# A scan and two expert layers on one core: a tile table after 24 blocks, eight first tiles half by half, and weight conversions tied to results

## The chip, the cores and the metric

The kernel runs on one core of a Trainium2 chip. The metric is device time in microseconds (us), the median of several runs. The engines named below are TensorE (PE, with its weight loads PEld), VectorE (DVE), ScalarE (ACT), GpSimd (POOL) and SyncE (SP). Each works through its own queue in order, and "SPq" or "ACTq" marks a transfer that the engine issues.

## The reference

Three steps follow one another over 10112 tokens of 256 numbers (two sequences of 5056). The first is a gated scan along the tokens; the other two are layers of eight experts in which each token goes to one expert.

```
f = lower_bound + (1 - lower_bound) * sigmoid(f_logit)
h[t] = f[t] * h[t-1] + (1 - f[t]) * x[t]              # along 5056 tokens
# layer 1: the expert is argmax of cosine(x, expert_emb) / tau
# layer 2: the expert is argmax of x @ w_gate
out[rows of e] = gate * (relu(x[rows of e] @ w1[e]) @ w2[e])   # w1: 256x1024, w2: 1024x256
```

## The kernel before

**Blocks and chunks.** The tokens are 79 blocks of 128. A chunk is two blocks, and there are 40. For each chunk the kernel loads `xf` (512 KB), forms the gate on ACT (tanh, then a scale and a bias on ACT or POOL), runs the scan on DVE (`p_scan`: one pass over 128x512 and two scans over 128x256), turns the result round on PE into two PSUM tiles `yt` (`p_mm`) and writes rows in two half-precision parts (`p_hi` on ACT, `p_lo` on DVE). Two chunks make a group of four blocks, a quad. For a quad small instructions choose the expert of each row (`p_top`, `p_rank`, `p_slot`, `p_up`), and four indirect transfers of POOL scatter the rows to a table in DRAM, ordered by expert (`p_put`, `X<-row,sl`).

**Tiles and units.** A tile is 128 rows of one expert. A checkpoint after so many blocks computes on DVE which tiles are sure to be full by then, and writes the numbers into `tab`; `cps` lists the blocks after which this is done (16, 32, 48 and 64, and once more at the end). The number of tiles known after 16, 24 and 32 blocks is 9, 17 and 25. A tile is computed in two units, one for each half of the 1024 hidden columns. A unit is a first matmul `mm1` (24 matmuls into `hps`), its result taken out of PSUM by ACT and then by DVE (`evac`, tile `hT`, below simply the result of the unit), and a second matmul `mm2` (12 matmuls into `ops`), which stands three units later in the order (`lag`). Each unit of a tile that is computed half by half loads its own transposed rows `xT`, into one of four buffers.

**Halves and weights.** The first `g0` tiles run half by half: first their first halves, one after the other, then their second halves. ACT adds the partial sums aside (`acc`). So units 0 to g0-1 need only the first-half weights. Weights arrive as 512 KB pieces in single precision, one for each expert, half and matrix, and are split into two half-precision parts: `w_hi` on ACT, then `w_lo` on DVE (four of the first pieces by PE and ACT, `wd`). In the rows W_0_102 is the first half of the first weights, W_1_103 the second half of them, W_0_104 the first half of the second weights, W_1_105 the second half of those. Pieces wait for their conversion in parts of these arrays that aren't used yet, or in three buffers `ws`. `w1` says at which unit the conversion of the second halves begins.

**Order.** Every step of chunks, weights and tiles is put at a unit number (a slot, below zero ahead of unit 0) with a priority; SP's queue then keeps the order in which the steps were written, and a scheduler orders the other engines up to unit 17. `hold` and `rates` give the first slot of each chunk. PSUM holds six buffers that `yt`, `wd`, `hps` and `ops` use in turn.

Of the kernel before, what the change touches and what calls it, by code (L numbers as in the profile page):

```python
# [14 lines left out]
ALU = mybir.AluOpType  # L15
# [9 lines left out]

CFG = {'cps': (16, 32, 48, 64),
 'g0': 4,
 'swap': 21,
# [9 lines left out]
 'gdve': 0,  # L38
 'wpe': (4, 0),
 'yg': (0, 0),  # L40
 'man0': ('SP',),
# [3 lines left out]
 'hold': (8, -9),  # L45
 'rates': ((17, 2), (99, 4)),
 'alias': 8,
 'mans': 17,
# [15 lines left out]
 'sc': (0, 26),  # L64
 'w1': (-8, 0.8),
 'w1s': (20, 0.8),
# [58 lines left out]
def scan_moe_moe_kernel(ctx, tc, xf, emb, cst, tmp, w1a, w2a, w1b, w2b, out, seq, cfg=CFG):  # L125
# [59 lines left out]
    def stt(eng, out, in0, s, in1, op0, op1, **kw):  # L185
        assert eng is V
        return eng.scalar_tensor_tensor(out=out, in0=in0, scalar=s, in1=in1, op0=op0, op1=op1, **kw)  # L187
# [526 lines left out]

    ring = {}

    wreg = [T.alloc_register(f"wa{i}") for i in range(16)]
# [66 lines left out]
    def evac(t, h):  # L784
        hps = t.pop("hps")
        hT = hp.tile([P, 8, P], F16, name="hT", tag="hT", bufs=LAG + 2)
        hh = hT.rearrange("p (a c) q -> p a (c q)", a=2)
        A.activation(out=hh[:, 0], in_=hps, func=ACTF.Relu)  # L788
        stt(V, hh[:, 1], hps, 0.0, hh[:, 0], ALU.max, ALU.subtract)
        t["hT", h] = hT  # L790
# [254 lines left out]
    s0 = {}  # L1045
    s = cfg["start"]
    for c in range(NCH):
        if c == cfg["hold"][0]:
            s = cfg["hold"][1]
        s0[c] = int(s)  # L1050
        s += next(r for n, r in cfg["rates"] if c < n)
    first = min(s0.values())
    for c in range(NCH):
# [8 lines left out]
        if 2 <= c < cfg["alias"]:  # L1062
            at(first - 2 + (c - 2) // 2, 2, p_load, c)
        elif c >= 2:
            pa("load", p_load, c)
# [29 lines left out]
    wps = {}  # L1095

    def wstep(load, hi, lo, lo2):
        def w_done(item):
# [6 lines left out]
        if lo is not None:  # L1105
            t = wbuf.pop(lo)
            nlo[0] += 1
            i, k = nlo[0], (cfg["wpe"] + (0, 0))[(nlo[0] - 1) // 16]
            if (i * k) // 16 != ((i - 1) * k) // 16:
                wps[lo] = (w_sub(lo, t), t)  # L1110
            elif 16 < i <= 32 and tablast:
                with tc.issue_after(tablast[0]):
                    w_lo(lo, t)
                w_done(lo)
            else:
                w_lo(lo, t)
                w_done(lo)
        if hi is not None:
            w_hi(hi, wbuf[hi])
        if load is not None:  # L1120
# [272 lines left out]
```

## Time and profile before

| what | value |
|---|---|
| median of 3 runs | 1062.96 us (1060.74 to 1066.65) |
| time of the profiled execution | 1052.77 us |
| span from its first to its last instruction | 1050.9 us |
| PE busy | 996.1 us, 95% of the span |
| DVE, ACT, POOL busy | 602.3, 529.2, 407.8 us |

The span is 1.87 us shorter than the time of the same execution, and that execution was 10.19 us faster than the median of the runs. A row of a timeline gives the start, the busy time, the engine, the line and the operation with its output and inputs; in square brackets stands how long the engine was idle before it and what ended that. Busy times of neighbours overlap a little, so the distance from one start to the next is the better price of an instruction in a full queue. "Granted clock" (PEclk) is the share of TensorE's full clock, 1.00 for 2.4 GHz and 0.5 for 1.2 GHz.

### The profile page before, as it was taken

How to read it: one execution, taken by the hardware profiler on the slowest of the kernel's cores; microseconds unless marked ns; L12 is line 12 of the kernel's file. 1: busy time of each engine (PE TensorE's matmuls, PEld its weight loads, DVE VectorE, ACT ScalarE, POOL GpSimd, SP SyncE). 2: the span in 40 equal slices, each digit the busy share in tenths (PEclk: the TensorE clock that was granted, in tenths of full speed). 3: DMA queues.
4: the chain of work that ended last, by engine and by line, in shares of the span. 5: the costliest groups of instructions: out<-in, count | busy, mean ns of one | idle time of the engine just before them, and what ended most of it. 6: DMA issues, size and time to landing. Idle time of an engine off the chain costs nothing. (4 is left out here: it accounts for less than half of the span.)

```text
span 1050.9 us, 36737 instructions
## 1 busy us (share of the span) xinstructions
PE 996.1 (95%) x13267; PEld 932.6 (89%) x13267; DVE 602.3 (57%) x1927; ACT 529.2 (50%) x1301; POOL 407.8 (39%) x666
## 2 busy tenths in 40 slices
PE   5557999999999999999999999999999999999997
PEld 4436889999999999999998999999999999999997
DVE  7988877787778777665449778443222222222221
ACT  6978555665655565665346466443333333333332
POOL 5834645666666565332002550243222222222222
PEclk9967999999999999999999999999999999999999
DMA  9798436777677673875479699653322222222220
GB/s 352 244 342 209 132 59 120 144 136 130 124 127 127 152 125 94 195 196 149 62 170 205 123 197 267 117 103 72 52 52 53 52 53 48 45 50 44 47 51 31
DMA packets 195612, 132.69 MB, mean 126 GB/s; under 512 B 169601, under 2 KB 172558, under 8 KB 195440
## 3 DMA queue, kind: packets, MB, share of 16 engines
q1 hardware_dynamic: 172384, 60.18, 29.7%
q10 hardware_dynamic: 11200, 38.62, 14.7%
q0 software_dynamic: 11856, 31.51, 11.7%
q8 instruction: 118, 1.93, 0.8%
q14 instruction: 54, 0.44, 0.2%
HBM read 58.89 MB, written 38.85 MB: 93 GB/s over the span
## 5 line engine op out<-in xcount | busy, mean ns | idle before, releaser
L780 PE MATMUL hps<-xT,W 128*128 128x128 f16 x7968 | 504.9, 220 | 6.9 <-DVE hT L187 3.1
L802 PE MATMUL ops<-W,hT 128*128 x3984 | 489.3, 272 | 1.6 <-ACT acc L806 0.9
L780 PEld LDWEIGHTS <-W 128*128 x7968 | 475.6, 98 | 16.0 <-issue 6.3
L187 DVE SCALAR_TENSOR_TENSOR hT<-hps,hT 128x512 f16<-128x512 f32 x332 | 228.6, 688 | 318.4 <-ACT hT L788 315.7
L802 PEld LDWEIGHTS <-hT 128*128 128x128 f16 x3984 | 374.3, 98 | 41.4 <-issue 2.0
L788 ACT ACTIVATE hT<-hps 128x512 f16<-128x512 f32 x332 | 198.0, 596 | 303.2 <-PE hps L780 284.0
L970 POOL DMA_INDIRECT out<-osum,ti x83 | 81.1, 977 | 291.4 <-ACT osum L966 189.5
L948 POOL DMA_INDIRECT X<-trow,tsl x83 | 97.1, 1170 | 53.2 <-DVE tsl L187 18.0
L638 POOL DMA_INDIRECT X<-row,sl x79 | 92.8, 1174 | 55.1 <-issue 37.7
L966 ACT ACTIVATE osum<-ops,exr 128x256 f32<-128x256 f32 x62 | 29.3, 473 | 47.0 <-PE ops L802 44.8
L195 POOL TENSOR_TENSOR lf<-exr,us 128x2 f32<-128x2 f32 (+1 forms) x42 | 9.7, 231 | 102.6 <-DMA W<-WD 44.0
L187 DVE SCALAR_TENSOR_TENSOR W<-ws,W 128x1024 f16<-128x1024 f32 x34 | 41.5, 1220 | 8.7 <-ACT W L373 8.7
L373 ACT ACTIVATE W<-ws 128x1024 f16<-128x1024 f32 x35 | 37.1, 1060 | 12.5 <-DMA ws<-w2b 8.6
L825 ACT ACTIVATE trow<-osum 128x256 f16<-128x256 f32 x83 | 34.9, 420 | 16.0 <-DMA X<-trow,tsl 7.6
L492 DVE TENSOR_TENSOR_SCAN xf<-xf 128x256 f32<-128x256 f32 (+3 forms) x64 | 42.8, 710 | 0.1
L507 PE MATMUL yt<-cs,xf 128*128 128x128 f32 x126 | 28.3, 303 | 15.2 <-DVE xf L492 10.2
L814 ACT ACTIVATE osum<-ops 128x256 f32<-128x256 f32 x58 | 22.2, 382 | 38.3 <-PE ops L802 38.3
L187 DVE SCALAR_TENSOR_TENSOR trow<-osum,tsc,trow 128x256 f16<-128x256 f32 x83 | 36.7, 481 | 4.1 <-ACT trow L840 3.2
L187 DVE SCALAR_TENSOR_TENSOR xf<-xf 128x512 f32<-128x512 f32 (+1 forms) x32 | 21.8, 681 | 26.7 <-POOL xf L192 19.9
L547 ACT ACTIVATE row<-yt,sc 128x256 f16<-128x256 f32 x79 | 33.5, 481 | 6.5 <-DVE sc L192 6.5
L840 ACT ACTIVATE trow<-osum,tsc 128x256 f16<-128x256 f32 x62 | 28.1, 500 | 16.5 <-DVE tsc L192 14.9
L187 DVE SCALAR_TENSOR_TENSOR row<-yt,sc,row 128x256 f16<-128x256 f32 x79 | 36.0, 472 | 0.2 <-ACT row L547 0.2
(149 smaller groups left out, 929.2 us busy)
## 6 DMA issues: line engine op xcount, KB each, us to landing
xf<-xf ACTq DMA_DIRECT2D x28, 512.0 KB
ws<-w1b ACTq DMA_DIRECT2D x16, 512.0 KB
ws<-w2b ACTq DMA_DIRECT2D x16, 512.0 KB
W<-w1a SPq DMA_DIRECT2D x11, 512.0 KB
W<-xf SPq DMA_DIRECT2D x8, 512.0 KB
ws<-w2a ACTq DMA_DIRECT2D x8, 512.0 KB
WD<-wq SPq DMA_DIRECT2D x8, 512.0 KB
W<-WD SPq DMA_DIRECT2D x8, 512.0 KB
```

The costliest lines, as they stand in the source:

```text
L187: return eng.scalar_tensor_tensor(out=out, in0=in0, scalar=s, in1=in1, op0=op0, op1=op1, **kw)
L373: A.activation(out=hi, in_=src, func=ACTF.Copy, scale=64.0)
L492: V.tensor_tensor_scan(out=t[:, k, lo:hi], data0=t[:, 2 + k, lo:hi], data1=t[:, k, lo:hi], initial=init, op0=ALU.mult, op1=ALU.subtract)
L547: A.activation(out=p["row"][:, o + i, 0:D], in_=yv(d["yt"][i]), func=ACTF.Copy, scale=p["sc"][:, o + i:o + i + 1])
L638: x_write(0, G.indirect_dma_start(out=X[0], out_offset=IndirectOffsetOnAxis(ap=p["sl"][:, i, 0:1], axis=0), in_=p["row"][:, i, :].bitcast( ...
L780: T.matmul(out=hps[:, c, :], lhsT=w, rhs=xt[:, a, :], start=(n == 0), stop=(n == 5))
L788: A.activation(out=hh[:, 0], in_=hps, func=ACTF.Relu)
L802: T.matmul(out=o, lhsT=hT[:, a + k, :], rhs=w[:, b * D:(b + 1) * D], start=(first and k == 0 and n == 0), stop=(last and k == 3 and n == 2))
L825: A.activation(out=d["row"][:, i, D:2 * D], in_=t["O"], func=ACTF.Square, scale=0.25, accum_out=d["ss"][:, i:i + 1])
L948: x_write(1, G.indirect_dma_start(out=X[1], out_offset=IndirectOffsetOnAxis(ap=sl[:, i, 0:1], axis=0), in_=d["row"][:, i].bitcast(I32), in ...
L966: A.activation(out=r, in_=o, func=ACTF.Copy, scale=ex0[:, 0:1])
L970: i = ins_of(G.indirect_dma_start(out=out, out_offset=IndirectOffsetOnAxis(ap=ti, axis=0), in_=r, in_offset=None, bounds_check=N - 1, oob_ ...
```

## The change

Five things are edited. (1) A checkpoint after 24 blocks is added, so that the table comes in steps of 9, 8 and 8 tiles where it came in steps of 9 and 16. (2) Eight tiles instead of four run half by half, so units 0 to 7 use the first-half weights and units 8 to 15 the second-half ones. (3) The conversion of the second halves begins four slots later, and the pieces of W_1_105 but the first are put behind results: the piece of expert e not ahead of the result of unit e - 2, or of unit 0. (4) Chunks 8 to 11 are loaded at slots -18, -17, -12 and -10; before, the slots were -11, -9, -7 and -5. (5) Chunks 12 to 20 begin at slots 0, 2, 5, 8, 11, 14, 17, 19 and 22; before, at -1, 1, 3, 5, 7, 9, 13, 17 and 21.

```diff
-CFG = {'cps': (16, 32, 48, 64),
- 'g0': 4,
+CFG = {'cps': (16, 24, 32, 48, 64),
+ 'g0': 8,
+ 'wbe': 2,
+ 'first': {12: 0, 13: 2, 14: 5, 15: 8, 16: 11, 17: 14, 18: 17, 19: 19, 20: 22, 21: 25},
+ 'loads': {8: -18, 9: -17, 10: -12, 11: -10},
- 'w1': (-8, 0.8),
+ 'w1': (-4, 0.8),
+    evs = []
-        A.activation(out=hh[:, 0], in_=hps, func=ACTF.Relu)
-        stt(V, hh[:, 1], hps, 0.0, hh[:, 0], ALU.max, ALU.subtract)
+        i = A.activation(out=hh[:, 0], in_=hps, func=ACTF.Relu)
+        evs.append((ins_of(i), ins_of(stt(V, hh[:, 1], hps, 0.0, hh[:, 0], ALU.max, ALU.subtract))))
-        s0[c] = int(s)
+        s0[c] = cfg["first"].get(c, int(s))
+        elif c in cfg["loads"]:
+            at(cfg["loads"][c], 2, p_load, c)
+    def behind(item, eng, other=None):
+        m, which, h, e = item
+        if (m, which, h) == (0, 1, 1) and e:
+            other = evs[max(0, e - cfg["wbe"])][eng is V]
+        return tc.issue_after(other) if other is not None else ExitStack()
-                with tc.issue_after(tablast[0]):
+                with behind(lo, V, tablast[0]):
-            w_hi(hi, wbuf[hi])
+            with behind(hi, A):
+                w_hi(hi, wbuf[hi])
```

On SP's queue, at the start of the program, the loads stood thus before (`xf` is a chunk, `w1a` and `w2a` are weight pieces):

```order
L360 DMA W_1_103<-w1a 128x1024 x8
L360 DMA W_1_103<-w2a 128x1024 x4
L451 DMA xf<-xf 128x1024
L360 DMA W_1_103<-w2a 128x1024
L360 DMA ws<-w2a 128x1024
L451 DMA xf<-xf 128x1024
L360 DMA ws<-w2a 128x1024
L360 DMA W_1_105<-w1a 128x1024
L360 DMA ws<-w2a 128x1024
```

Now the same place of SP's queue reads:

```order
L363 DMA W_1_103<-w1a 128x1024 x4
L454 DMA xf<-xf 128x1024
L363 DMA W_1_103<-w1a 128x1024
L454 DMA xf<-xf 128x1024
L363 DMA W_1_103<-w1a 128x1024 x3
L363 DMA W_1_103<-w2a 128x1024 x3
L454 DMA xf<-xf 128x1024
L363 DMA W_1_103<-w2a 128x1024 x2
L454 DMA xf<-xf 128x1024
L363 DMA ws<-w2a 128x1024 x2
```

Chunks 8 and 9 have moved ahead of four pieces of the first weights, and chunks 10 and 11 stand among those of the second weights.

On DVE, from the result of unit 0 (the first `hT`) to that of unit 1 (the second), the queue before is this (`xf` are scan passes, `W_1_105` is a conversion, `er`, `oh`, `ri`, `lg` choose experts):

```order
L187 SCALAR_TENSOR_TENSOR hT<-hps,hT 128x512
L192 TENSOR_SCALAR sc<-pi 128x2
L195 TENSOR_TENSOR lg<-lg,mx 128x32
L187 SCALAR_TENSOR_TENSOR xf<-xf 128x512
L187 SCALAR_TENSOR_TENSOR er<-lg,cs 128x32
L492 SCALAR_TENSOR_TENSOR xf<-xf 128x256 x2
L581 TENSOR_REDUCE m_1006<-er 128x4
L187 SCALAR_TENSOR_TENSOR xf<-xf 128x512
L195 TENSOR_TENSOR oh<-er,m_1006 128x32
L187 SCALAR_TENSOR_TENSOR W_1_105<-ws,W_1_105 128x4x256
L593 RECIPROCAL ri<-ri 128x4
L187 SCALAR_TENSOR_TENSOR hT<-hps,hT 128x512
```

Now, from the result of unit 0 on, and as far as that of unit 2:

```order
L190 SCALAR_TENSOR_TENSOR hT<-hps,hT 128x512
L495 SCALAR_TENSOR_TENSOR xf<-xf 128x256 x2
L198 TENSOR_TENSOR er<-RK,oh 128x32
L190 SCALAR_TENSOR_TENSOR W_1_105<-ws,W_1_105 128x4x256
L596 RECIPROCAL ri<-ri 128x4
L190 SCALAR_TENSOR_TENSOR W_1_105<-ws,W_1_105 128x4x256
L615 TENSOR_REDUCE sl<-er 128x4
L190 SCALAR_TENSOR_TENSOR hT<-hps,hT 128x512
L198 TENSOR_TENSOR lg<-lg,ri 128x32
L190 SCALAR_TENSOR_TENSOR W_1_105<-ws,W_1_105 128x4x256
L190 SCALAR_TENSOR_TENSOR hT<-hps,hT 128x512
```

The two passes over 128x512 have gone from between the first two results, and one conversion more has come in. Further on, the rows of the new checkpoint (`ci`, `ct`, `le`, `tab`, 21 small instructions) stand between the results of units 2 and 6.

## Rows read from the trace of the kernel before

**Rows 1.** The page: its span, and PE's busy tenths in 40 slices.

```profile
span 1050.9 us, 36737 instructions
...
PE   5557999999999999999999999999999999999997
```

**Rows 2.** Busy time by stretches around the first unit: length, five engines, clock, DMA.

```profile
core 0: us, PE busy (x) PEld busy (x) DVE busy (x) ACT busy (x) POOL busy (x), PEclk, DMA share, GB/s
40.00:60.00 20.00, 13.79 (x52) 7.31 (x51) 17.59 (x57) 15.17 (x29) 16.59 (x14) 0.91 0.75 265
60.00:82.77 22.77, 12.23 (x51) 8.59 (x51) 17.79 (x38) 19.56 (x46) 3.01 (x6) 0.58 0.87 284
82.77:87.66 4.89, 4.89 (x49) 4.89 (x50) 4.89 (x9) 4.89 (x15) 2.40 (x1) 0.52 0.79 269
87.66:117.41 29.75, 23.20 (x260) 20.69 (x257) 25.14 (x66) 20.06 (x55) 17.51 (x21) 0.94 0.74 175
117.41:154.79 37.38, 35.44 (x463) 32.70 (x462) 28.05 (x115) 21.29 (x69) 18.31 (x27) 1.00 0.36 91
```

**Rows 3.** Timeline of PE: units 0 and 1, unit 3, and unit 4's second matmul.

```profile
82.77 5.06 PE L780 MATMUL hps<-xT,W 128*128 128x128 f16 x48
...
94.94 2.72 PE L780 MATMUL hps<-xT,W 128*128 128x128 f16 x24 [3.07 <-DVE hT L187]
...
117.41 1.47 PE L802 MATMUL ops<-W,hT 128*128 x12
```

**Rows 4.** Timeline of PE at full rate: a chunk, a second and a first matmul.

```profile
122.91 0.41 PE L507 MATMUL yt<-cs,xf 128*128 128x128 f32 x2
...
124.14 0.18 PE L429 MATMUL RK<-oh,tri 128*128 128x32 f16 x1
...
147.91 1.47 PE L802 MATMUL ops<-W,hT 128*128 x12
149.22 1.50 PE L780 MATMUL hps<-xT,W 128*128 128x128 f16 x24
150.56 0.17 PE L429 MATMUL RK<-toh,tri 128*128 128x16 f16 x1
```

**Rows 5.** Timeline of DVE between the results of units 0 and 4.

```profile
87.92 0.68 DVE L187 SCALAR_TENSOR_TENSOR hT<-hps,hT 128x512 f16<-128x512 f32 x1
...
89.42 1.38 DVE L492 TENSOR_TENSOR_SCAN xf<-xf 128x256 f32<-128x256 f32 x2
90.72 0.16 DVE L581 TENSOR_REDUCE m<-er 128x4 f32<-128x32 f32 x1
...
94.14 0.18 DVE L593 RECIPROCAL ri<-ri 128x4 f32<-128x4 f32 x1 [1.42 <-POOL ri L191]
...
106.49 0.84 DVE L187 SCALAR_TENSOR_TENSOR row<-yt,sc,row 128x256 f16<-128x256 f32 x2
107.25 0.68 DVE L187 SCALAR_TENSOR_TENSOR xf<-xf 128x512 f32<-128x512 f32 x1
107.85 1.21 DVE L187 SCALAR_TENSOR_TENSOR W<-ws,W 128x1024 f16<-128x1024 f32 x1
108.98 0.18 DVE L187 SCALAR_TENSOR_TENSOR er<-lg,cs 128x32 f32<-128x32 f32 x1
109.09 0.68 DVE L187 SCALAR_TENSOR_TENSOR hT<-hps,hT 128x512 f16<-128x512 f32 x1
```

**Rows 6.** Timeline of DVE ahead of unit 0: a wait, and quad 4's rank.

```profile
70.84 1.23 DVE L187 SCALAR_TENSOR_TENSOR W<-W,W 128x1024 f16<-128x1024 f32 x1 [2.42 <-ACT W L373]
...
78.15 0.19 DVE L195 TENSOR_TENSOR er<-RK,oh 128x32 f32<-128x32 f32 x1 [0.26 <-PE RK L431]
```

**Rows 7.** Timeline of ACT: a weight load issued, and the conversion that waited for it.

```profile
55.03 0.33 ACTq L360 DMA_DIRECT2D W<-w1a  x1
...
69.75 1.06 ACT L373 ACTIVATE W<-W 128x1024 f16<-128x1024 f32 x1 [1.94 <-DMA W<-w1a]
```

**Rows 8.** The table X, 20 to 130 us: how long its scatters took to land.

```profile
DMA to landing us min/median/max: 2.9/4.9/7.6
```

## The prediction

> **What bounds the kernel now.** I read the page first: PE is 90% busy or more from the fifth of forty slices to the last but one, and half busy in the first three [rows 1]. So only the start can give much, and the start is read by stretches. Unit 0 begins at 82.77 us. In the 22.8 us ahead of it PE is busy 12.2 us at a granted clock of 0.58, while ACT is busy 19.6 and DVE 17.8 [rows 2]: ACT and DVE are what unit 0 waits for, since they convert weights, scan chunks and choose experts in one queue each.
>
> After unit 0 I compare what PE did with what it could do. At full rate a first matmul takes 1.34 us (149.22 to 150.56), a second 1.31 us (147.91 to 149.22), a chunk's `yt` 1.23 us (122.91 to 124.14) [rows 4]. By 117.41, where unit 4's second matmul starts [rows 3], PE had done 8 first matmuls (10.7 us), 4 second ones (5.2), 4 chunks (4.9) and about 0.8 us of small ones: 21.7 us of work in 34.6 us. 12.9 us were lost there. From 117.41 to 154.79 it did 10 first and 11 second matmuls (13.4 and 14.4), 3 chunks (3.7) and, as an estimate, 2.5 us of small ones and turns: 34.0 in 37.4 us [rows 2], a loss of 3.4.
>
> Where the 12.9 us went is seen on three timelines. Units 0 and 1 took 4.9 us for 2.7 us of work, because the clock was at 0.52, the 1.2 GHz level [rows 2, 3]. Then unit 3 stood 3.07 us for a result on DVE [rows 3]. On DVE the results of units 0 and 4 start 21.2 us apart, at 87.92 and 109.09 [rows 5], though four units are worth 10.6 us of PE.
>
> **The change: DVE's queue between results.** This is the main term. DVE's prices, start to start, are 0.60 us for a pass over 128x512 (107.25 to 107.85; a result has that size too), 1.30 for a pair of scans (89.42 to 90.72), 1.13 for a conversion (107.85 to 108.98), 0.38 for a `row` (106.49 to 107.25, two) and 0.1 for a small one (108.98 to 109.09) [rows 5]. From the result of unit 0 to that of unit 4 the order before has 4 results, 4 passes, 3 scan pairs, 5 conversions, 4 rows and 20 small ones: 2.4 + 2.4 + 3.9 + 5.65 + 1.5 + 2.0 = 17.9 us. The other 3.3 us of the 21.2 are waits, 1.42 of them for POOL's `ri` [rows 5]. The order after has 4 results, no pass, 1 scan pair, 4 conversions, 2 rows and 19 small ones (10 of them the new table's): 2.4 + 1.3 + 4.5 + 0.8 + 1.9 = 10.9 us. The chunks have gone ahead of unit 0 or behind, and the later slots thin them out.
>
> What is late next I find by laying this beside PE, with time 0 at unit 0 and the same 3.3 us of waits. Result 0 starts 5.2 us after unit 0, as now (82.77 to 87.92) [rows 3, 5]. Result 4 then ends at 5.2 + 10.9 + 0.6 + 3.3 = 20.0. PE has 8 first and 4 second matmuls and 3 chunks ahead of unit 4's second matmul, 20.5 us of work with the small ones, plus 2.2 us at the low clock: ready at 22.7, no wait. Between results 4 and 5 DVE's queue has 5.8 us (a scan pair, two passes, a conversion, 16 small ones, a result), so result 5 ends at 25.8; PE is ready at 25.4. Between 5 and 6 there are 5.3 us more, so result 6 ends at 31.1; PE is ready at 28.6 and waits 2.5 us. Results 7 and 8 follow 0.7 and 1.2 us after. So I put the loss after the change at 2.2 (clock) + 2.5 (result 6) + 1.0 (an estimate for what a refilling queue loses) = 5.7 us in place of 12.9, and of the 3.4 us behind it I let half stay, for waits there don't all come from DVE. Gain: 12.9 - 5.7 + 1.7 = 8.9 us.
>
> **When unit 0 starts.** In both orders the same 12 chunks and five quads stand ahead of unit 0 on PE. Before, the last was chunk 11's `yt`; after, it is quad 4's rank, which follows `er<-RK` on DVE. That instruction ran at 78.15 [rows 6]. In the new order DVE has about 4.0 us more ahead of it: a chunk more (0.60 + 1.30), a conversion (1.13), and some rows and small ones. Against that, DVE loses 2.42 us before it in a wait for ACT, whose conversion had waited 1.94 us for a load [rows 6, 7]. With the wait kept unit 0 starts at 78.15 + 4.0 + 0.4 = 82.6, without it at 80.1. I take a gain of 1.1 us, near the middle of 0.2 to 2.6.
>
> **Loads.** Four chunk loads (0.52 MB each) move ahead of or among weight loads. That the DMA engines have room for them is read in the stretch from 40 to 60 us, where the share is 0.75 at 265 GB/s; from 60 to 82.77 it is 0.87 at 284 [rows 2]. Chunks 10 and 11 take a buffer that the rows of quads 0 and 1 must leave, so SP may stand there until a scatter has landed, 2.9 to 7.6 us after its issue [rows 8]; behind SP stand the last pieces of W_0_104. They are converted on ACT some 8 us of work later than before, which covers it. Without that cover up to 4 us would come to unit 0's second matmul. The Trainium skill, DMA: Bandwidth & Descriptors, "Issuing engines are not separate DMA queues", says that transfers of all queues run on the same 16 engines and interleave. By that a load moved up only pushes others back, and bringing chunks up is no gain; by the row, a share of 0.75, there is room. It is the second rival below that this rule would speak for.
>
> **What costs nothing.** The four more partial sums (`acc`) on ACT and sums on DVE lie in a stage in which ACT is 57% busy from 117.41 on [rows 2]. The eight conversions behind results need their loads through three `ws` buffers; a load that lands as the scatters do (2.9 to 7.6 us) reaches the fifth conversion on ACT about when result 4 is due, 3 us ahead of PE's need. If it took 14.7 us, as the weight load from 55.03 to 69.75 did [rows 7], result 4 would be 4 to 7 us late. The work taken out between results (chunks 12 to 20, at most five slots later) goes to units 12 and up, where PE is busy 35.4 of 37.4 us with DVE at 75% [rows 2]. The tables come earlier in units of work than they are used: tile 9 is needed at unit 18, and the 24-block table is ready by result 6.
>
> **Sum.** 8.9 + 1.1 = 10.0 us less: 1042.8 us for an execution like the profiled one (1052.77, with 1.87 us around its span). The median of the runs lies 10.19 us above that execution; I take the difference off the median and predict 1053 us.
>
> **Rivals.** *The table takes the place of the chunks.* Results 5 and 6 have 11.1 us of queue between them and result 4, for two units that are worth 5.3 us. If the waits on POOL's `ri` stretch from 3.3 to 8 us, PE stands 4.7 us more, and unit 0 starts no earlier: 10.0 - 4.7 - 1.1 = 4.2 us gained, 1059. For it speaks the wait of 1.42 us [rows 5], against it that POOL's first step for quad 5 now stands ahead of quad 4's four scatters.
>
> *The loads only change places.* Two chunks ahead of the first weights are 1.05 MB; at 284 GB/s [rows 2] they hold back the conversions by 3.7 us. Then unit 0 starts 3.7 us later than I take it: 10.0 - 3.7 = 6.3, 1056.5. The half-idle stretch from 40 to 60 speaks against it, since the chunks would have come through by then.
>
> *The transposed loads pace the halves.* This one ends slower. Now sixteen units in a row load an `xT` each into four buffers; before it was eight. A load starts when the unit four ahead of it has ended its first matmul, so four units take a landing time plus about 2.5 us of issue and matmul. They are worth 10.6 us on PE, so it decides from a landing time of 8 us. At the 14.7 us that a weight load took in a full stretch [rows 7] four units take 17.2 us, and units 4 to 15 lose 3 times 6.6, 19.8 us: 1053 + 19.8 = 1073. For it speaks that share of 0.74 from 87.66 to 117.41; against it the 0.36 behind it [rows 2] and the scatters' 4.9 us [rows 8].
>
> *It doesn't do what it says* can be left out, since the order shows the instructions moved.
>
> **The numbers.** Runs of this kernel lie 6 us apart, so 0.5% (5.3 us) is about the least that can be told from no change. The forecast (6 to 14 us gained) has 0.52, more than 14 gained 0.06, the loads 0.14, the table 0.18, the transposed loads or something like it 0.10. Faster by over 0.5% takes in the forecast, the best case, and two thirds of the loads: 0.67; within 0.5%: 0.24; slower: 0.09. The range takes in the loads and the table with a thin gain of 1 us, and at the other end unit 0 at 80.1 with all of the 16.3 us but the clock's 2.2 given back (16.6 gained): 1046 to 1062.
>
> **What would show it.** In the profile after, the results of units 0 and 4 start 14 us apart on DVE, not 21; unit 4's second matmul starts about 23 us behind unit 0; PE's one wait of over 2 us is at unit 6; unit 0 starts between 80 and 83. If unit 0 is late, the loads were not free; if PE waits in even steps for `xT` at units 4 to 15, the third rival holds; if the gaps sit at units 5 and 6 and are over 5 us, the table does. Were PE's idle time after 160 us to grow, moved work would have come back there, which no part of this sum has.

## The result, and the profile after

The kernel after took 1076.77 us (median of 4 runs, 1073.39 to 1081.14), the kernel before 1063.03 (4 runs, 1060.74 to 1066.65): a ratio of 1.013, 95% interval 1.0095 to 1.0164. It is slower; 1053 us was forecast. Its profiled execution took 1077.14 us.

The page of the kernel after, against [rows 1]: the span, and the tenths of PE and of its clock in 40 slices.

```profile
span 1075.4 us, 36817 instructions
...
PE   5668898999999999999999999999999999999997
...
PEclk9967899999999999999999999999999999999999
```

The stretches of [rows 2], cut at the same events (unit 0 at 80.98, unit 4's second matmul at 115.45, unit 18 at 155.36):

```profile
core 0: us, PE busy (x) PEld busy (x) DVE busy (x) ACT busy (x) POOL busy (x), PEclk, DMA share, GB/s
40.00:60.00 20.00, 15.01 (x48) 8.26 (x48) 14.19 (x58) 13.74 (x31) 9.62 (x13) 0.74 0.94 326
60.00:80.98 20.98, 9.94 (x43) 6.64 (x44) 20.98 (x41) 19.57 (x46) 5.67 (x7) 0.65 0.65 185
80.98:86.06 5.08, 5.08 (x48) 5.08 (x49) 4.96 (x16) 5.08 (x10) 4.29 (x4) 0.50 0.67 169
86.06:115.45 29.39, 22.02 (x239) 19.64 (x237) 22.19 (x66) 17.18 (x44) 8.43 (x12) 0.85 0.95 185
115.45:155.36 39.91, 38.55 (x441) 34.17 (x442) 25.94 (x96) 20.23 (x63) 15.55 (x22) 0.93 0.36 94
```

The loads have moved: 326 GB/s from 40 to 60 us where it was 265, and 185 behind it where it was 284. Unit 0 starts 1.8 us earlier. From unit 0 to unit 4's second matmul it takes 34.5 us, as long as before (34.6), with one chunk less to do, at a DMA share of 0.95. PE's timeline there, against [rows 3]:

```profile
80.98 5.28 PE L784 MATMUL hps<-xT,W 128*128 128x128 f16 x48 [0.48 <-ACT lg L530]
...
91.14 1.47 PE L806 MATMUL ops<-W,hT 128*128 x12
...
99.38 2.72 PE L806 MATMUL ops<-W,hT 128*128 x12 [3.50 <-ACT acc L810]
...
109.48 1.96 PE L784 MATMUL hps<-xT,W 128*128 128x128 f16 x24 [1.16 <-DMA xT<-X]
...
114.25 0.69 PE L510 MATMUL yt<-cs,xf 128*128 128x128 f32 x2 [2.15 <-ACT acc L810]
...
115.45 2.72 PE L806 MATMUL ops<-W,hT 128*128 x12
```

Unit 0's second matmul comes 10.2 us after unit 0 (16.4 before, the row below), and unit 3 no longer waits for a result.

```profile
99.19 1.63 PE L802 MATMUL ops<-W,hT 128*128 x12 [0.15 <-DVE sl L612]
```

But unit 1's second matmul waits 3.50 us for an `acc` of ACT and then runs at half clock (2.72 us for 1.47), and so does unit 4's after a wait of 2.15. DVE's results, against [rows 5] (units 0, 1, 4, 5 and 6):

```profile
85.35 0.68 DVE L190 SCALAR_TENSOR_TENSOR hT<-hps,hT 128x512 f16<-128x512 f32 x1
...
91.02 0.68 DVE L190 SCALAR_TENSOR_TENSOR hT<-hps,hT 128x512 f16<-128x512 f32 x1
...
99.09 1.23 DVE L190 SCALAR_TENSOR_TENSOR W<-ws,W 128x1024 f16<-128x1024 f32 x1 [4.02 <-ACT W L376]
...
101.51 0.68 DVE L190 SCALAR_TENSOR_TENSOR hT<-hps,hT 128x512 f16<-128x512 f32 x1
...
107.63 0.68 DVE L190 SCALAR_TENSOR_TENSOR hT<-hps,hT 128x512 f16<-128x512 f32 x1
...
114.62 0.68 DVE L190 SCALAR_TENSOR_TENSOR hT<-hps,hT 128x512 f16<-128x512 f32 x1
```

Results 0 and 4 start 16.2 us apart (21.2 before, 14 forecast). The queue has shrunk as counted; 4.02 us of what is left is one wait of a conversion for ACT. What ACT was doing:

```profile
92.72 0.60 ACT L792 ACTIVATE hT<-hps 128x512 f16<-128x512 f32 x1 [0.66 <-PE ops L806]
97.62 0.33 ACTq L363 DMA_DIRECT2D ws<-w2a  x1
98.00 1.06 ACT L376 ACTIVATE W<-ws 128x1024 f16<-128x1024 f32 x1 [4.68 <-DMA exr<-X]
98.97 0.36 ACT L810 ACTIVATE acc<-ops 128x256 f32<-128x256 f32 x1
...
104.45 1.06 ACT L376 ACTIVATE W<-ws 128x1024 f16<-128x1024 f32 x1 [0.99 <-DMA ws<-w2a]
...
108.57 1.06 ACT L376 ACTIVATE W<-ws 128x1024 f16<-128x1024 f32 x1 [1.33 <-DMA ws<-w2a]
...
112.39 1.06 ACT L376 ACTIVATE W<-ws 128x1024 f16<-128x1024 f32 x1 [1.75 <-DMA ws<-w2a]
```

ACT did nothing for 4.68 us. It stood at the issue of a `ws` load (97.62), which counts on a semaphore that the small load `exr` had used before it; SP had issued that `exr` at 89.84, and it landed at 97.55:

```profile
89.84 0.41 SPq L766 DMA_DIRECT2D exr<-X  x1
```

The conversions behind it each waited for their own load, and `acc` and the results stood behind them.

By unit 18 PE is still level with before (0.6 us later). By unit 60 it is 13.9 us later and at the end 24.5. Some 10 of these 24.5 belong to the other side of the comparison, since the profile of before is 10.2 us faster than the median of its kernel. This is PE's timeline of the kernel after at units 22 to 25, where before had no idle time:

```profile
170.81 0.53 PE L784 MATMUL hps<-xT,W 128*128 128x128 f16 x5
172.65 1.22 PE L784 MATMUL hps<-xT,W 128*128 128x128 f16 x19 [1.31 <-issue]
...
181.43 0.66 PE L806 MATMUL ops<-W,hT 128*128 x4
182.47 0.27 PE L806 MATMUL ops<-W,hT 128*128 x1 [0.38 <-issue]
183.21 0.38 PE L806 MATMUL ops<-W,hT 128*128 x2 [0.47 <-issue]
184.88 0.71 PE L806 MATMUL ops<-W,hT 128*128 x5 [1.30 <-issue]
185.57 2.52 PE L784 MATMUL hps<-xT,W 128*128 128x128 f16 x24
```

Matmuls of one group, which wait for nothing of another engine, come a few at a time ("issue"), and the unit at 185.57 behind them runs at half clock. I call these gaps. In the profile of before there was none after unit 0. In this one there are 20 of over 0.15 us, 12.6 us in all.

### The profile page after: what moved, and what is told of

It is laid out like the page before. It is cut to its first block, busy times and chain, and to the rows that moved or that the text cites. A ratio compares the mean times of both kernels' runs of the same rounds, so it can differ in the third digit from the quotient of the medians.

```text
span 1075.4 us, 36817 instructions
## 1 busy us (share of the span) xinstructions
PE 1010.5 (94%) x13283; PEld 940.3 (87%) x13283; DVE 602.2 (56%) x1952; ACT 527.5 (49%) x1305; POOL 398.8 (37%) x666
## 5 line engine op out<-in xcount | busy, mean ns | idle before, releaser
L784 PE MATMUL hps<-xT,W 128*128 128x128 f16 x7968 | 511.4, 220 | 12.3 <-issue 7.1
L806 PE MATMUL ops<-W,hT 128*128 x3984 | 496.1, 274 | 7.2 <-ACT acc L810 3.5
L784 PEld LDWEIGHTS <-W 128*128 x7968 | 478.9, 99 | 25.2 <-issue 12.2
L641 POOL DMA_INDIRECT X<-row,sl x79 | 85.6, 1083 | 56.4 <-issue 28.8
L195 POOL TENSOR_SCALAR xf<-xf,fa,fb 128x256 f32<-128x256 f32 (+1 forms) x48 | 26.3, 553 | 43.0 <-ACT xf L461 27.9
L829 ACT ACTIVATE trow<-osum 128x256 f16<-128x256 f32 x83 | 35.0, 422 | 10.8 <-DVE osum L198 5.4
L818 ACT ACTIVATE osum<-ops 128x256 f32<-128x256 f32 x54 | 20.7, 384 | 33.6 <-PE ops L806 29.0
L512 PEld LDWEIGHTS yt<-cs,xf 128*128 128x128 f32 x252 | 36.7, 210 | 0.0
```

Of the source, the lines that this page charges most:

```text
L512: T.matmul(out=yt[:, D:D + E], lhsT=t[:, k, i * P:(i + 1) * P], rhs=ide[:, (1 - k) * (P + E):(1 - k) * (P + E) + E], start=(k == 0), stop= ...
L641: x_write(0, G.indirect_dma_start(out=X[0], out_offset=IndirectOffsetOnAxis(ap=p["sl"][:, i, 0:1], axis=0), in_=p["row"][:, i, :].bitcast( ...
L784: T.matmul(out=hps[:, c, :], lhsT=w, rhs=xt[:, a, :], start=(n == 0), stop=(n == 5))
L806: T.matmul(out=o, lhsT=hT[:, a + k, :], rhs=w[:, b * D:(b + 1) * D], start=(first and k == 0 and n == 0), stop=(last and k == 3 and n == 2))
L829: A.activation(out=d["row"][:, i, D:2 * D], in_=t["O"], func=ACTF.Square, scale=0.25, accum_out=d["ss"][:, i:i + 1])
```

## The experiments

The median of before lay between 1054.7 and 1065.8 us from chip to chip, so the comparison stands only within one. The five used behind the result are called B to F, with before's median. Each was met in one batch of runs, so what belongs to the chip and what to the batch can't be told apart. The table has the start of units in us against the profile of before shown above, read from the first of a unit's 24 `hps` matmuls. The last two columns are the number of gaps after unit 0 and their sum in us.

```
unit                  0      8     18     32     60    120    200   gaps
before    B        +0.3   +1.6   +1.8   +1.8   +1.8   +1.2   +5.4    2  3.7
before    E        -0.1   -1.0   -0.3   -0.3   -0.3   +0.2   +2.6    0
before    F        -0.7   -2.1   -1.0   -0.2   -0.2   +3.0   +9.8    7  3.3
after     result   -1.8   -0.8   +0.6  +13.4  +13.9  +18.4  +24.5   20 12.6
after     C        -3.8   -3.6   -6.4   -1.8   -1.4   -2.3   -5.2    1  0.3
after     D        -1.6   -5.0   -3.7   +7.8   +8.8  +13.9  +25.8   20 10.2
after     E        -1.5   -2.0   -3.7   +1.0   +1.3   +0.4   +5.1    1  1.9
after     F        -0.7   -2.0   -0.9  +12.0  +12.3  +15.3  +22.1   19 11.0
no tie    C        -3.9  -10.9  -12.8   -7.9   -7.9   -8.0   +2.6    0
exr POOL  C        -4.4  -11.2  -10.1   -0.5   +5.8   +6.0  +15.8    1  2.8
old slots B        -5.2   -1.6   -2.7   -1.0   -1.0   -1.8   +1.2    0
4 halves  B        -6.3   -4.5   -6.1   -4.1   -4.1   -4.9   +2.0    2  2.4
4 halves  D        -4.4   -6.0   -4.7   -0.9    0.0   +3.7   +1.3   11  5.7
no loads  B        +0.8   +3.5   +2.0   +6.7   +6.7   +6.4  +12.7    0
no loads  D        -0.2   +2.9   +4.3  +18.9  +19.3  +24.5  +31.3   20 10.7
loads     D        -5.0   -2.1   -0.5   +0.5   +1.0   +3.7   +2.3   13  5.6
tab+loads C        -4.9   -1.1   -2.4   -2.4   -2.4   -3.3   +2.1    0
64 more   E        -1.6   +1.7   -0.2   +4.5   +4.5   +3.9  +13.0    2  2.9
8 halves  E        +0.4   +5.6   +4.5   +6.2   +6.2   +8.0  +11.4    0
```

From unit 18 to 32 the kernels with late slots and eight halves take 4.7 to 4.9 us longer than before even without gaps. They do 56 matmuls more there, some 3.7 us: the `yt` of one chunk, 24 `x2p` (layer-1 rows turned for layer 2), and small ones. Another 1.0 us is waits, about half of it for an `x` of ACT. The chunk stood ahead of unit 18 before, but 16 of the `x2p` PE doesn't do at all in before (156 in the whole program, 172 with eight halves). So part of a lead at unit 18 is only work put off, and a gain at the start is read at unit 60.

### One part undone at a time (chip B, before 1057.17)

Before, unchanged: 

> The kernel before, unchanged, profiled a second time. The two profiles so far differ in two ways: the kernel after has gaps of 0.2 to 1.3 us inside groups of matmuls (idle time ended by 'issue', not by another engine), some 12 us of them and what goes with them between 160 and 200 us and some 8 us between 290 and 360, and the kernel before has none there. Theory F (the gaps belong to executions, not to the change): this profile has a span of about 1061 us, near the median, and gaps inside groups of matmuls that sum to 5 us or more between 100 and 400 us. Theory L (they come from the change): PE has no such gaps here between 150 and 400 us, and the span is 1051 us, or is longer for another reason.

 It took 1058.07 us and had no gap between 150 and 400 us. That is theory L. It spoke for the change as the only cause of the gaps, which chip F will correct.

The slots of chunks 12 to 20 as before:

```diff
- 'first': {12: 0, 13: 2, 14: 5, 15: 8, 16: 11, 17: 14, 18: 17, 19: 19, 20: 22, 21: 25},
+ 'first': {},
```

> The kernel after with chunks 12 to 20 back at the slots of before (-1 to 21); table after 24 blocks, eight halves, conversions behind results and early loads kept. Theory L (the chunk work taken out of the first units comes back at units 18 to 30, where PE then waits): most of the 13.7 us come back, 1062 to 1067 us, ratio to before 1.000 to 1.004, and unit 30 starts less than 15 us after the place it has before. Theory S (the loss is made by the eight halves with their partial sums and conversions): 1074 to 1080 us, ratio 1.010 to 1.016, since the chunks' passes stand between the results again.

 1058.37 us, ratio 1.0012 (0.9985 to 1.0039). The ratio is theory L's, but the next chip takes away what it was measured against.

The chunk loads as before:

```diff
- 'loads': {8: -18, 9: -17, 10: -12, 11: -10},
+ 'loads': {},
```

> The kernel after with chunks 8 to 11 loaded as before (slots -11, -9, -7, -5). Theory D (the chunk loads hold back weights, xT or their conversions): unit 0 starts 1 us or more earlier than at 80.98 us, or the waits for acc and xT in units 1 to 8 shrink, and the time falls to 1066 to 1070 us (ratio 1.003 to 1.007). Theories S and L: unit 0 starts later (82 to 84 us), and the time stays at 1075 to 1081 us (ratio 1.011 to 1.017).

 1066.37 us, ratio 1.0087 (1.0057 to 1.0118); unit 0 at 83.54, as theories S and L have it, with a ratio between theirs and theory D's. The early loads don't hold units back. Theory D falls.

Four halves, no tie:

```diff
- 'g0': 8,
+ 'g0': 4,
- 'w1': (-4, 0.8),
+ 'w1': (-8, 0.8),
-        if (m, which, h) == (0, 1, 1) and e:
+        if cfg['wbe'] and (m, which, h) == (0, 1, 1) and e:
- 'wbe': 2,
+ 'wbe': 0,
```

> The kernel after with four tiles half by half again (g0 4), the conversion of the second halves at slot -8 and no conversion put behind a result; table after 24 blocks, slots of chunks and early loads kept. Theory S (the eight halves and what hangs on them lose the time): 1061 to 1066 us, ratio 0.998 to 1.003, and no wait of PE for acc over 1 us. Theory L: 1074 to 1079 us, ratio 1.010 to 1.015, with PE's idle time again between units 20 and 30.

 1050.89 us, ratio 0.9935 (0.9908 to 0.9963), lower than either theory had it. I took from these three that eight halves cost 2%. That sum left out that the kernel after itself had not been run on this chip.

### The kernel after again (chip C, before 1054.69)

The kernel after, unchanged: 

> The kernel after, unchanged, beside the others on one chip. The first profile of it had 21 gaps of PE over 0.15 us between 120 and 420 us, 16 of them inside a group of matmuls, 10.1 us in all; no other profile had more than 5. Theory G (the gaps belong to this kernel, through where its instructions are fetched): they are here again, 5 us or more in all, and the ratio to before is 1.011 to 1.016. Theory C (they were chance of one execution, and the loss is in the start and in the waits behind it): under 2 us of them, a span of about 1068 us, and a ratio of 1.007 to 1.012 as without the early loads.

 1051.79 us, ratio 0.9973 (0.9942 to 1.0005), one gap. Neither theory had this: twelve runs, none above 1058.73, where the four of the result had none under 1073.39.

Table and early loads alone (four halves and no tie as above, old slots): 

> Only the table after 24 blocks and the early loads: four halves, conversion of the second halves at slot -8 and not tied to results, chunks 12 to 20 at their old slots. It is the fourth corner of a square with the kernel after (1.013), without the late slots (1.001) and without the eight halves (0.9935). Theory A (the two losses add up, 1.2% and 2%): 0.981 to 0.985. Theory I (they only hurt together, since both fill the same stretch with loads): 0.991 to 1.000, that is, no better than without the eight halves alone.

 1050.41 us, 0.9963 (0.9933 to 0.9993). That is theory I's figure. But on this chip the kernel after is within its interval, so there is no 2% of the eight halves to be found here, and no square.

The tie alone undone:

```diff
-        if (m, which, h) == (0, 1, 1) and e:
+        if cfg['wbe'] and (m, which, h) == (0, 1, 1) and e:
- 'wbe': 2,
+ 'wbe': 0,
```

> The kernel after with its eight conversions of W_1_105 no longer put behind results. Theory B (the tie puts a conversion whose load is late ahead of results and partial sums in ACT's queue): PE's wait of 3.5 us for acc at unit 1's second matmul is under 1 us, and the ratio falls to 1.003 to 1.008. Theory R (the loads of ws themselves are late, tie or not): ratio 1.010 to 1.017, and the wait for acc or for a result stands at the same place, within 2 us of its length.

 1052.85 us, 0.9978 (0.9947 to 1.0009), below both theories, as the kernel after itself is on this chip. The stretches from unit 0 to 8, and from 8 to 18, without the tie and then with it, both on chip C:

```profile
78.84:107.86 29.02, 26.28 (x300) 23.84 (x301) 27.09 (x81) 21.59 (x54) 14.19 (x15) 0.92 0.87 212
107.86:142.04 34.18, 33.83 (x429) 30.87 (x427) 25.70 (x98) 19.39 (x61) 16.51 (x22) 1.00 0.63 118
```

```profile
78.97:115.12 36.15, 29.18 (x297) 26.02 (x298) 28.08 (x82) 22.98 (x56) 13.48 (x15) 0.83 0.97 193
115.12:148.35 33.23, 33.04 (x430) 30.68 (x428) 24.55 (x94) 19.42 (x60) 16.10 (x22) 1.00 0.42 94
```

Eight units take 29.0 us instead of 36.2, and unit 4's second matmul comes 27.6 us after unit 0 instead of 33.6. The landing times of the loads say why. Those of the last five `ws` loads of `w2a` in each profile, about unit 0 and behind it, from issue to the last count on their semaphore, median and longest in us:

```
before (4 profiles)             4.8 to 6.1    longest 8.0
after (5: result, C, D, E, F)   10.8  11.2  8.9  6.9  10.4    longest 15.0
no tie (C)                      5.0           longest 6.3
old slots (B)                   6.3           longest 7.7
four halves (B)                 6.6           longest 9.7
eight halves alone (E)          6.5           longest 12.6
```

A tied conversion holds its buffer, the next load waits for the buffer, and the loads then go out together with those of two chunks and four scatters. On this chip the last four `ws` loads are issued at 86.56, 89.98, 90.47 and 97.43 us with the tie, at 79.22, 84.12, 89.56 and 93.10 without; the two chunk loads go out from 86 to 90 in both, four scatters from 92 to 97 with the tie, and from 80 to 86 and again from 98 on without. The same 512 KB land in half the time without the tie. With the tie and the old slots they landed in 6.3 us too, so both seem to be needed. Theory B holds for the start: the run without the tie is 6.5 us ahead at unit 60. Yet the total is the same (1052.85 and 1051.79 us): from unit 120 to 190 this profile loses 13.7 us of PE's time, the kernel after on this chip 1.1. These are one execution each, the one without the tie 2.4 us above its median, the other 4.4 below.

`exr` issued by POOL, with a register of its own there:

```diff
-            i = SP.dma_start(out=ex, in_=X[m].bitcast(F32)[ds(r, P), 256:258])
+            r = reg_load("rg", G, (key, j), 1, DUM)
+            i = G.dma_start(out=ex, in_=X[m].bitcast(F32)[ds(r, P), 256:258])
```

> The kernel after with the small loads exr issued by POOL instead of SP. In the profile after, ACT stands from 93.32 to 97.62 us at the issue of a load of ws that waits for a semaphore which exr, issued at 89.84 and landed at 97.55, used before it. Theory S (the shared semaphore holds ACT): ACT's wait is under 1 us, PE's wait of 3.5 us for acc is gone, the time falls by 3 to 6 us (ratio 1.007 to 1.010). Theory R (the transfers of 90 to 104 us land 7 to 17 us after their issue whatever they wait for): the conversion behind it then waits for its own load and the ratio stays at 1.010 to 1.017.

 1069.98 us (6 runs), 1.0149 (1.0105 to 1.0193). Theory S is right on the start: PE loses 0.7 us of idle time up to unit 8 (7.0 with `exr` on SP), and unit 8 comes 7.6 us earlier. It is wrong on the total, which lies where theory R had it: 15.9 us go between units 18 and 60, 4.7 of them as in the other kernels. POOL now issues `exr` between its scatters and its gate work for the rest of layer 1; that this is what costs is a guess, and not shown.

### A chip with gaps (chip D, before 1065.76)

The kernel after, unchanged: 

> The kernel after, unchanged, a third time. Its first four runs stood at 1.013 of before, twelve runs on another chip at 0.997, without the gaps inside groups of matmuls. Theory P (the first chip had slow transfers and late instructions, and the change itself does little): 0.994 to 1.003 here, gaps inside groups under 2 us. Theory Q (this kernel has two manners of running, and which one it falls into is drawn anew each time it is loaded): either 0.994 to 1.003 or 1.009 to 1.017 with gaps of 5 us and more, and nothing between.

 1078.99 us, 1.0116 (1.0081 to 1.0152): the result again, with 20 gaps. Theory Q, in its second branch. That it is drawn at each loading is not what the table suggests, since the kernels of one chip go together.

The chunk loads as before, again: 

> The kernel after with chunks 8 to 11 loaded as before, again, now beside the kernel after itself. Theory L (the early loads are worth it: with them unit 0 started at 77 to 81 us in six profiles, without them at 83 to 84): ratio to before 1.005 to 1.011, and 5 to 11 us above the kernel after beside it. Theory P (the 1.0087 was the chip's): within 3 us of the kernel after.

 1084.30 us, 1.0169 (1.0130 to 1.0207), 5.3 us above the kernel after: theory L at its lower bound, on a chip where both ratios are higher than it had them.

Four halves, no tie, again: 

> Table, early loads and late slots, with four halves and no tie, again. Theory I (the eight halves cost a little at units 0 to 18 and nothing elsewhere): ratio 0.991 to 0.996, 2 to 5 us under the kernel after beside it. Theory P: within 2 us of the kernel after.

 1062.34 us, 0.9973 (0.9948 to 0.9997), 16.7 us under the kernel after, where both theories had at most 5; the ratio is a little above theory I's. It has gaps too, but 5.7 us of them, and none at units 22 to 25.

The early loads alone, on the kernel before:

```diff
+ 'loads': {8: -18, 9: -17, 10: -12, 11: -10},
...
-        elif c >= 2:
+        elif c in cfg["loads"]:
+            at(cfg["loads"][c], 2, p_load, c)
+        elif c >= 2:
```

> The kernel before with one edit: chunks 8 to 11 loaded at slots -18, -17, -12 and -10. Theory L (the loads are the part of the change that gains): unit 0 starts at 76 to 79 us instead of 83, and 3 to 6 us of that last to the end: ratio 0.994 to 0.997. Rival (what is gained at unit 0 is waited for at units 0 to 18, since tables and second weights don't come sooner): ratio 0.998 to 1.002.

 1061.89 us, 0.9979 (0.9956 to 1.0001). Unit 0 comes 5 us earlier, and 0.5 us later than before by unit 32: between theory and rival, and nearer to the rival.

### Before and after side by side (chips E, 1056.43, and F, 1064.46)

On chip E: 

> The kernel before, profiled once more, on the chip of the next three. On the chip where the kernel after was 1.2% slower, all four profiles had gaps ended by 'issue' inside groups of matmuls (10.2 us in the kernel after, 10.7 without the early loads, 5.7 with four halves, 5.6 with the early loads alone); on the two chips where before stood at 1055 to 1057 us the sums were 0 to 3.7 us. Theory H (the chip makes the gaps, the change makes them dearer): if before stands near 1064 us here, this profile has 4 to 7 us of gaps and the kernel after 9 or more; if it stands near 1056, both have under 4 us.

 

> The kernel after, profiled beside before. Theory H: gaps of 9 us or more, the largest at units 22 to 30 as in its first and third profile, if before has 4 us or more here; else under 4 us. Rival (the gaps belong to the kernel after): 9 us or more whatever before shows.

 1055.29 and 1057.74 us, one execution each, gaps of 0 and 1.9 us: theory H for a chip without gaps.

64 more small matmuls ahead of all:

```diff
-        T.matmul(out=RK, lhsT=ones16, rhs=s0, start=True, stop=True, skip_group_check=True)
+        for _ in range(65):
+            T.matmul(out=RK, lhsT=ones16, rhs=s0, start=True, stop=True, skip_group_check=True)
```

> The kernel after with 64 more small matmuls at the very start, where PE has nothing else to do: every later instruction of PE stands 128 places further on in its stream, and nothing else changes. Theory J (the gaps depend on where an instruction stands in the stream): on a chip with gaps they stand elsewhere than in the kernel after, or have another sum (a difference of over 4 us), and the ratio moves by over 0.4%. Theory K (they depend on the work, that is, on what else is moving then): the same gaps at units 22 to 30, the sum within 3 us, and the ratio within 0.4% of the kernel after on such a chip (1.012). On a chip without gaps both expect 0.995 to 1.000.

 1059.46 us, 1.0009 (0.9978 to 1.0041), 2.9 us of gaps. It met a chip without gaps at units 22 to 30, so it doesn't decide between J and K.

The kept traces do, in part, when PE's instructions are counted from its first, weight loads and its sequencer's included: 29943 in the kernel before, 29969 in the kernel after, 30097 here. The profile of the kernel after on the result's chip and the six profiles on D and F, of five kernels in all, have gaps in unit 99 and ahead of the 18th to 20th matmul of unit 106. That place in unit 106 is number 10814 to 10819 in the kernels with four halves and 10841 to 10845 in the others, and it came at 425 to 448 us. These gaps go with the work, as theory K has it, and the kernel before has them too.

Single longer gaps of another kind, seven of 0.97 to 3.54 us, stand at 475 to 592 us in profiles from the result's chip, B, C and E. They come at different matmuls, but always at number 12390, 15207, 15462 or 15463. These are multiples of 256 apart to within one, as theory J would have it. The page's queue q8, "instruction", brought 118 packets, one for every 254 of PE's instructions, and each of these gaps ended 1.3 to 2.0 us behind the end of one. That PE waited there for its instructions is likely, and not shown.

Eight halves, tie and later conversion alone (slots, loads and table of before): 

> The kernel before with eight halves, the second halves' conversion at slot -4 and tied to results; loads, slots and table as before. Theory M (eight halves are what costs on a chip with gaps, by themselves): 1.008 to 1.018 there, 0.998 to 1.006 on a chip without. Theory I (they cost only with the late slots and the early loads): 0.997 to 1.004 on either.

 1060.43 us, 1.0025 (1.0001 to 1.0050): both theories allow it on such a chip. Its profile has no gap, and yet it is 6.5 us behind that of before on this chip at unit 60. All of this is lost by unit 8, 7.0 us in one wait of PE for an `acc`, with `ws` loads of up to 12.6 us:

```profile
107.28 1.01 PE L784 MATMUL hps<-xT,W 128*128 128x128 f16 x8 [6.96 <-ACT acc L810]
```

So eight halves with the tie cost at the start without the late slots and the early loads, too.

On chip F: 

> The kernel before, profiled a fourth time, beside the kernel after on one chip. Theory H (the chip makes the gaps, the change makes them dearer): on a chip where before stands at 1063 us or more it has 4 to 7 us of gaps ended by 'issue' after unit 0, fewer than the kernel after; where it stands at 1058 us or less, under 4 us.

 

> The kernel after beside it. Theory H: where before stands at 1063 us or more, a ratio of 1.010 to 1.015 and 9 us of gaps or more; where it stands at 1058 us or less, a ratio of 0.995 to 1.002 and gaps under 4 us. Against H would be a ratio of 1.008 or more on a chip without gaps, or under 1.005 on a chip with them.

 Before took 1062.44 us, the kernel after 1073.70, ratio 1.0082 (1.0050 to 1.0113), a little under what H asked for. PE's waits from unit 0 on, rows "issue" (us in total, times, longest), of before and then of after:

```profile
PE hps L780 <- issue: 2.2, 5, 0.5
...
PE ops L802 <- issue: 1.1, 2, 0.7
```

```profile
PE hps L784 <- issue: 9.2, 16, 1.2
...
PE ops L806 <- issue: 1.8, 3, 1.1
```

The kernel before has gaps on this chip too, 3.3 us of them (H had 4 to 7), and the kernel after 11.0. Units 18 to 32, before and then after:

```profile
153.83:197.82 43.99, 43.59 (x606) 41.22 (x604) 32.57 (x123) 25.44 (x83) 25.49 (x42) 1.00 0.64 130
```

```profile
153.85:210.03 56.18, 49.80 (x662) 45.98 (x660) 37.09 (x157) 31.05 (x102) 30.51 (x53) 0.97 0.45 105
```

Both begin at the same time. After, the stretch is 12.2 us longer: 4.7 are the 56 matmuls (662 and 606 in the rows) and the 1.0 us of waits that the kernel has without gaps too, and most of the rest is PE's idle time (6.4 in all, 0.4 before) and the clock (0.03 of 56, 1.7). The two spans lie 12.3 us apart (1060.7 and 1073.0). So some 4.7 us of that are the start's, where less was done by unit 18 and it came no earlier, and some 7.5 are gaps and the clock behind them. The gaps stand where they stood in the result's profile, here the first matmul of unit 22 and the second matmul ahead of unit 25:

```profile
169.28 0.44 PE L784 MATMUL hps<-xT,W 128*128 128x128 f16 x4
170.86 1.28 PE L784 MATMUL hps<-xT,W 128*128 128x128 f16 x20 [1.14 <-issue]
...
180.64 0.38 PE L806 MATMUL ops<-W,hT 128*128 x2 [0.36 <-issue]
181.36 0.49 PE L806 MATMUL ops<-W,hT 128*128 x3 [0.34 <-issue]
182.97 0.60 PE L806 MATMUL ops<-W,hT 128*128 x4 [1.12 <-issue]
```

## Why the prediction was wrong

Two steps failed: one on the start, one on the total. Beside them stand gaps that no step had.

**The failed step on the start is "What costs nothing".** It took the conversions behind results (it counts eight; the edit ties seven) as free, from loads that land in 2.9 to 7.6 us, and said that loads of 14.7 us would make result 4 late by 4 to 7. They took up to 12.5 us here (the median of the five is 10.8, and 6.9 to 11.2 over five profiles). Result 4 itself was only 1.2 us later than counted (21.2 us after unit 0, forecast 20.0); what was late was the partial sum behind the conversion on ACT (3.50), a transposed load (1.16) and the sum again (2.15), and the half clock after two of them, so that unit 4's second matmul came 34.5 us after unit 0 instead of 23. The prediction read ACT's room for partial sums off the stretch from 117.41 on (57% busy); the waits for them ended at 99.38 and 114.25, ahead of it. Without the tie it came after 27.6 (33.6 with it on that chip).

Better prices stood in the trace of before. The 14.7 us of [rows 7] pair two different loads: the conversion at 69.75 waited on the semaphore of a load that SP had issued at 52.17, the row below, and that took 17.6 us; the one that ACT issued at 55.03 had landed at 62.88. And `ws` loads themselves took 4.6 to 7.6 us about unit 0 and behind it, but 8.3, 11.0 and 14.4 us where three of them went out among other loads from 46.66 to 48.85.

```profile
52.17 0.33 SPq L360 DMA_DIRECT2D W<-w1a  x1
```

The Trainium skill, DMA: Bandwidth & Descriptors, "Issuing engines are not separate DMA queues", has it that transfers of all issuers share the same engines; the trace agrees, since a 1 KB `exr` on SP's queue took 7.7 us beside the loads that ACT had issued (at most 4.6 in before). The prediction held that rule against the early chunk loads, which did no harm, and not against the `ws` loads, which did.

**Main term, 8.9 us, and the sum, 10.0.** DVE's queue did shrink (results 0 and 4 16.2 us apart, 14 forecast). PE's loss from unit 0 to 18 (idle time, and the time lost at half clock; the prediction's 12.9 and 3.4 us, counted by full-rate prices, are some 4 more) was 11.9 to 14.3 us in four profiles of before and 10.9 to 17.3 in five of after, so nothing was gained. It was 5.4 without the tie. At unit 60 the kernel without the tie is 7.9 us ahead of the profile of before, which wasn't taken beside it. So DVE's queue was the right mechanism and its term about right in size, on condition of the step that failed; that rests on one profile.

**The failed step on the total is the sum: that a gain at the start stays.** It carried the gain to the end as it stood. But with the failed step undone, and the start 6.5 us ahead, the time is the same: 1052.85 us without the tie, 1051.79 with it. The run without the tie had 8.0 us at unit 120 and none at unit 200; the early loads alone had 5.0 at unit 0 and none at unit 32. Between units 120 and 190, where the second layer begins, PE lost 3.5 to 10.0 us in four profiles of before and 1.1 to 15.0 in five of after. Whether an earlier start makes that wait longer, or it only scatters, isn't shown; the equal medians of the kernels with and without the tie speak for the first, as far as one profile of each goes. The cause of this part stays open.

**Work moved behind unit 12.** It did little harm by itself: one chunk more between units 18 and 32, beside the `x2p` of the eight halves, and 1.0 us of waits there on chips without gaps, where before has none. The prediction's alarm, idle time after 160 us, did go off, for the most part for another reason.

**The gaps** were in no step, and no row of the profile of before could show one: it fell on a chip without them, or so its 1052.77 us and the runs of 1060.74 to 1066.65 suggest. They go with the sign of the result: where before stood at 1063 to 1066 us the ratio was 1.013, 1.0116 and 1.0082; where it stood at 1055 it was 0.9973, an interval that takes in 1; and on a fourth (1056) one execution each lay 0.2% apart, and the kernel after with 64 small matmuls more had 1.0009 in 12 runs. In the one pair of profiles on F they and the clock behind them are some 7.5 us of 12.3, and the kernel after has three times the gaps of before. On D the excess goes with the eight halves, tie and later conversion: without them the same kernel has half the gaps and is 16.7 us shorter. What makes the gaps, and by what the eight halves add to them, is open, since from unit 16 on both do the same tiles in the same order.

**Unit 0.** Gain forecast 1.1, between 80 and 83 us; it started at 78.97 to 82.08 in five profiles of after (mean 80.9) and at 82.06 to 83.05 in four of before (82.6): 1.7. **Loads.** Better than forecast at unit 0: alone they bring it forward by 5 us. The rival that they "only change places", with unit 0 later by 3.7 us, falls; of the time they alone gain 0.2% (0.9956 to 1.0001). **The table** rival falls too: results 5 and 6 came 6.1 and 7.0 us after the one before, but PE waited for other things. **The transposed loads**: the only rival on the right side. It decided from a landing time of 8 us; from unit 0 to 8 their median was some 5 to 8 us in the five profiles of after, with single ones of 10 to 17.5, and some 3 to 4 behind. PE waited for them 1.16 us in the result's profile, once each on C (3.1) and E (2.0), and in no even steps. So it isn't the mechanism, and that its 1073 us lies near the measured 1076.77 is luck, though what it named, loads that come late through full queues, is what failed.

The best version of those tried has table, early loads and late slots but four halves and no tie: 0.9935 of before on chip B and 0.9973 on D. The kernel after was run beside it on D alone, and is 16.7 us slower there.

## What to carry to other kernels

An instruction that waits for a load is free only if the queue behind it is: before tying conversions to results, price what stands behind them on that engine, and price their loads at what such loads take when everything else is issued in the same few microseconds. Run a small change on several chips before believing its sign, with before beside it each time; here the same two kernels were 1.3% apart on one chip and no further apart than the noise on another. A gain at the start counts only when it is still there behind the next stretch that waits.

## What the hardware showed that was not expected

PE stood still inside groups of matmuls on some chips and not on others, for nothing that the profile shows. A few instructions came at a time, often some 0.7 us from one piece to the next (182.47 to 183.21 above). In the kernel after this happened in the same units on three chips (22, 24, 99 and 106 on each), and there on none of two others. A gap can cost twice: in each of the three profiles one or two stretches at half clock followed, in the result's that of the unit at 185.57 (2.52 us for 1.50).

A load can wait for one that has nothing to do with it. In this program the loads on SP's and ACT's queues share eight semaphores, taken about in turn, and the `ws` load at 97.62 went out only when the last user of its semaphore had landed (97.55). The Trainium skill, DMA: Bandwidth & Descriptors, "Why a DMA increments its semaphore by 16 and not by 1", says that with two transfers in flight on one semaphore a wait for the first can pass before all of it has landed; no run here shows that. That the program waits for this reason is my reading; the trace shows the price, 4.3 us of ACT (93.32 to 97.62) for a 1 KB load.
